# Maxima of the last 64 queries in one block-diagonal product, a slot softmax with other operations, and new order numbers for the attention stage

## The chip, the cores and the metric

One core of a Trainium2 chip runs the whole program. The time is the device time of one execution in microseconds (us). Five engines work side by side: TensorE (PE, with its weight loads as PEld), VectorE (DVE), ScalarE (ACT), GpSimd (POOL) and SyncE (SP, which issues the DMAs).

## The reference, cut to what matters

Attention over 4 batches with 8 heads, 1152 tokens and head size 64, the queries averaged in pairs to 576; then a soft mixture of experts with 32 slots; then a dense layer pair with `h - tanh(h)` between.

```python
q_pool = q.reshape(B, H, S // 2, 2, D).mean(axis=3)
scores = scale * np.matmul(q_pool, k.transpose(0, 1, 3, 2))
scores = scores - np.max(scores, axis=-1, keepdims=True)
attn = np.exp(scores); attn = attn / (np.sum(attn, axis=-1, keepdims=True) + 1e-09)
x = attn @ v                                   # [2304, 512] after the heads are laid side by side
logits = x @ phi                               # 32 slots
d = softmax over tokens (axis 0); slot_input = d.T @ x
slot_out[e] = relu(slot_input[e] @ w1[e]) @ w2[e]
c = softmax over slots (axis 1);  x = c @ slot_out
h = x @ w_in;  out = (h - tanh(h)) @ w_out
```

## The kernel before, in words

**Pairs and steps.** Two heads of one batch form a pair: head 0 lies in partitions 0 to 63, head 1 in 64 to 127. There are 16 pairs, four to a batch. A pair has 18 steps: two halves of 288 queries, nine chunks of 128 keys each. One step of `attend` computes the scores of its chunk for both heads (L556, eight matmuls, which are four products of 64x128 weights per head that use half of the array's rows each, so that the two heads run side by side), takes the exponential on ACT (L568), adds it to a running sum on POOL (L609, on DVE in the last pair) and multiplies it with V (L590, four matmuls per step, each using half of the array's columns). The products with V are issued for 2, 2, 2, 2 and 1 steps at a time (`PV_END`), so five groups to a half. `normalise` sums the running sums over the partitions (L633) and divides.

**Maxima.** The largest score of each query must be known before its scores are computed, because it enters them as the fourth product (`one`, `MX`). `smax` finds it one pair ahead: for each of five blocks `t` of 128 queries and three thirds `g` of the keys it computes the scores of both heads coarsely (L464, two matmuls side by side) and reduces each head's on DVE (L478). 576 queries are four and a half blocks, so the fifth block starts at query 448 and repeats 64 queries of the fourth. `smax_end` reduces over the thirds (L491), transposes (L494) and writes the rows with ten small DMAs a pair (L501): six for the first part (blocks 0 to 2), four for the second (blocks 3 and 4).

**Tiling modes.** TensorE thus works in different shapes of the array: 64x128 (L556, L464), 128x64 (L590, L633), 128x32 (L699, L805, L809) and the full array, 128x128 (L784, L733).

**Slots.** After each batch `moe_batch` computes the logits (L699), an online softmax over tokens (`mx`, `ee`, `ssum`), transposes x and the exponentials (L784, L733), adds to the slot inputs (L805, L809), and makes the softmax over slots for the second use: `c1` (L826 maximum, L827 subtraction), `c2` (L832 exponential), `c3` (L838 sum, L839 plus 1e-9, L840 reciprocal, L841 multiplication). The last batch ends in `combine`. `convert` (L996 to L1030) turns the float64 weights of the last layer into float32 during attention, 32 pieces, and keeps the split form in memory.

**What sets the order.** Nothing in the attention stage is issued in program order. Each piece of work is an `op` with the engines it can run on, a cost, the slots of memory it needs (seven PSUM banks `ps`, with caps of `st` 6 for scores, `sm` 4 for maxima and `ms` 4 for the rest; eight buffers `P` of exponentials) and a number `prio`. `Plan.run` plays the whole stage through on paper: an engine that is free takes the ready op of the lowest number, and on PE, among ops within `SLACK` of the lowest, one that needs no change of mode. A change of mode costs `TURN` on paper. The order so found is written out as each engine's fixed queue; on the chip only semaphores hold it up. Numbers count steps (pair i begins at 18 i) plus an offset from `PR`: the scores of step s stand at s - 2.62, the products with V at s + 0.73.

**After attention** (from L1203) come the expert weights' products (L1251, L1330), whose weights are loaded by DMA as buffers come free, and the dense layers (L1460, L1505).

Of the kernel before, what the change touches and what calls it, by code (L numbers as in the profile page):

```python
# [32 lines left out]
class Plan:  # L33
# [15 lines left out]
    TURN = 190.0  # L49
# [7 lines left out]
    def op(self, engs, fn, prio, deps=(), take=(), use=(), dma=0, alone=None,  # L57
           mode=None):

        o = {
            "n": len(self.ops), "engs": engs, "fn": fn, "prio": prio, "take": tuple(take),
            "use": tuple(use), "dma": dma, "deps": 0, "next": [], "done": False, "alone": alone, "mode": mode,
            "ready": dict.fromkeys(engs, 0.0),
        }
# [20 lines left out]
    def run(self):  # L87
# [20 lines left out]
        while left:  # L108
            progress = True
            while progress:  # L110
                progress = False
                for e in engines:
# [48 lines left out]
                    free_at[e] = end = now + o["engs"][e]  # L161
                    if e == "PE" and o["mode"] not in (None, self.mode):
                        self.mode = o["mode"]
                        free_at[e] = end = end + self.TURN
# [30 lines left out]
def fused_kernel(  # L195
# [12 lines left out]
    nc = tc.nc  # L208
# [39 lines left out]
    PB = 8  # L248
    NXT = 5
    PV_END = (1, 3, 5, 7, 8)  # L250
    CAP_ST, CAP_SM, CAP_MS = 6, 4, 4
    PR = {
# [5 lines left out]
    }  # L258
    tags_w = [f"W{n}" for n in range(NWR)]
    tags_b = [f"B{n}" for n in range(21)]  # L260
# [44 lines left out]
    mrun = cp.tile([128, 2], F32, name="mrun")  # L305
# [11 lines left out]
    MT = [mo.tile([128, 32], F32, name=f"mt{n}") for n in range(4)]  # L317
    one = mo.tile([128, 128], F32R, name="one")
    LOC = ((0, 64), (64, 128))

    def halves(tag):
# [3 lines left out]
    P_buf = [x for n in range((PB + 1) // 2) for x in halves(tags_b[(14, 15, 16, 20, 21)[n]])]  # L325
# [4 lines left out]
        "mc": 2, "k": 1, "v": 2, "q": 1, "rs": 1, "raw": 1, "cv": 1, "x": 1, "cw": 1, "hl": 1,  # L330
    }, PR["sw"])
# [12 lines left out]
    def act(n, sb=0, ptr=0):  # L344
        return {"ACT": 0.8333 * n + 51 + 42 * sb + 93 * ptr}
# [4 lines left out]
    def pool_tt(n):  # L350
        return {"POOL": 2.11 * n + 147}
# [50 lines left out]
    def split(i, what, out, parts, prio):  # L402
# [4 lines left out]
        for n, (c, end, key) in enumerate(parts):  # L407
# [17 lines left out]
            lo = op({"DVE": 1.0417 * w + (700 if i else 67)}, fl, prio + PR["lo"] + (0 if i else PR["late"]), deps=[hi], use=[sl])  # L425
# [20 lines left out]
    QOFF = (0, 128, 256, 384, NQ - 128)  # L446
    PARTS = ((0, 1, 2), (3, 4))
    mc_t, mx_t, mx_m = {}, {}, {}

    def smax(i, part, t, g, prio):  # L450
        a = i % 2
# [3 lines left out]
        msl, n0 = mc_t[i, part], PARTS[part].index(t)  # L455
        c0, q0 = g * KW, QOFF[t]
        deps = ready[i, "k", g][0] + ready[i, "q", 0][0]
        if q0 + 128 > HQ:
            deps = deps + ready[i, "q", 1][0]
        bk = [psum("sm") for _ in range(2)]  # L460

        def f(_):
            for (lo, hi), (ps, _) in zip(LOC, bk):
# [7 lines left out]
        m = op(pe(171), f, prio, deps=deps + mx_m[i, part][:1], mode=ROW2,  # L471
               take=both + ([msl] if first else []), use=both + [msl])
        mx_m[i, part].append(m)
        for h, (ps, pst) in enumerate(bk):
            n = h * len(PARTS[part]) + n0

# [5 lines left out]
            mx_t[i, part].append(op(dve(KW), red, prio, deps=[m], use=pst + [msl]))  # L482

    def smax_end(i, part, prio):
        a = i % 2
        w = len(PARTS[part])
# [3 lines left out]
        def f1(_):  # L490
            nc.vector.tensor_reduce(  # L491
                out=mn[:, 0:2 * w], in_=msl.tile[:, 0:2 * w], axis=AX.X, op=ALU.max, negate=True
# [3 lines left out]
        def f4(_):  # L496
            m = MX[a].bitcast(F32)
            for h in range(2):
                for n, t in enumerate(PARTS[part]):
                    b0 = 2 if t == 4 else 0  # L500
                    nc.sync.dma_start(  # L501
                        out=m[64 * h:64 * h + 1, QOFF[t] + 32 * b0:QOFF[t] + 128],
                        in_=mt[32 * b0 + h * w + n:128:32, :],
                    )

        o1 = op(dve(150), f1, prio, deps=mx_t.pop((i, part)), use=[msl])
# [3 lines left out]
        ready[i, "m", part] = op({"SP": 600.0 * 2 * w}, f4, prio, deps=[o1] + war, dma=4000)  # L510

    def prepare(i, g0):
        def at(key):
            return g0 + PR[key] + (0 if i else PR["first"])

        load(i, "k", at("k"))
        load(i, "q", at("q") - (0 if i else 10))
        load(i, "v", at("v"))
        sum_q(i, at("sum"))
        a = i % 2  # L520
        if i:
            split(i, "q", (QH[a], QL[a]), ((0, NQ, (0, 1)),), at("q0"))
            split(i, "k", (KH[a], KL[a]), ((0, CK, (0, 1, 2)),), at("k0"))
        else:
            split(i, "q", (QH[a], QL[a]), ((0, HQ, (0,)), (HQ, NQ, (1,))), at("q0"))
            split(i, "k", (KH[a], KL[a]), [(g * KW, g * KW + KW, (g,)) for g in range(3)], at("k0"))
        n = 0
        for t in range(3):
            for g in range(3):
                smax(i, 0, t, g, at("m0") + PR["m0d"] * n)  # L530
                n += 1
        smax_end(i, 0, at("e0"))
        for n in range(6):
            smax(i, 1, 3 + n // 3, n % 3, at("m1") + PR["m1d"] * n)
        smax_end(i, 1, at("e1"))
# [5 lines left out]
    def attend(i, s):  # L541
        a = i % 2
        hf, c = divmod(s, NCH)
        g = i * NSTEP + s
# [19 lines left out]
        m = op(pe(520), mm, g + PR["st"], deps=deps, take=both, use=both, mode=ROW2)  # L564
        last_read.setdefault((i, "T"), []).append(m)
        for h, (st, stt) in enumerate(bk):
# [5 lines left out]
            exps.append(op(act(HQ), ef, g + PR["ex"], deps=[m] + exps, take=[] if h else [psl],  # L572
# [7 lines left out]
        if c in PV_END:  # L580
# [4 lines left out]
            def pvf(_):  # L585
# [10 lines left out]
                pe(490 * len(run)), pvf, g + PR["pv"],  # L596
# [17 lines left out]
        if i == NPAIR - 1:  # L614
            engs = dve(2 * HQ)
        acc_last[i, hf] = op(
            engs, add, g + PR["add"],
            deps=exps + (e0 if c == 1 else [acc_last[i, hf]]),
            take=[acc] if c == 1 else [], use=[acc, psl] + ([p0] if c == 1 else []))

    def normalise(i, hf, prio):
# [39 lines left out]
        def ev(_):  # L661
            nc.scalar.activation(out=posl.tile, in_=pvs.tile[:, :HQ], func=AF.Copy)

        oe = op(act(HQ), ev, prio + PR["ev"], deps=[o_pv[i, hf]], take=[posl], use=[pvs, posl])
        o = op(pe(490), sums, prio, deps=[acc_last[i, hf]], take=pst, use=pst + [acc], mode=COL2)
        acc_read[i, hf] = o
        o = op(act(HQ, 0, 1), ln, prio, deps=[o], take=[rsl], use=pst + [rsl])
        o = op(act(HQ, 1), rc, prio, deps=[o], use=[rsl])
        o = op(dve(HQ), n1, prio, deps=[o], use=pst + [rsl])
        o = op(dve(HQ), n2, prio, deps=[o], use=pst + [rsl])  # L670
        xdone.append(
            op(dve(HQ), n3, prio, deps=[o, oe], take=[] if hf else [xsl],
# [10 lines left out]
    def moe_batch(b, g0, dg, last):  # L683
# [5 lines left out]
        prio = [g0 + n * dg for n in range(12)]  # L689
        kinds = ("ms", "sm", "st", "ms", "sm", "st", "ms", "ms") if last else ("ms",) * 8  # L690
        (psL, ptL), (psT, ptT), (psU, ptU), (psS, ptS) = (psum(kinds[n]) for n in range(4))
        new, old = mrun[:, b % 2:b % 2 + 1], mrun[:, 1 - b % 2:2 - b % 2]
# [917 lines left out]
```

## Time and profile before

| | us |
|---|---|
| median of 3 runs | 757.57 |
| the runs | 755.52 to 760.40 |
| span of the profiled execution (first to last instruction; the page gives it no other time) | 753.6 |
| busy PE, DVE, ACT, POOL in the span | 726.4, 652.8, 485.9, 379.8 |

Attention fills the span up to about 470 us, the experts up to about 530 us, and the dense layers the rest. A busy share of an engine says that something was under way on it, not that it was at its peak: a matmul's row lasts longer than the distance to the next one, since they are pipelined. So distances on PE are read from start to start.

### The profile page before, as it was taken

To read this page: it belongs to the slowest core of one execution; us is meant where nothing else is said; L and a number is where in the kernel's file an instruction comes from. 1 tells how busy PE (TensorE), PEld (TensorE's weight loads), DVE (VectorE), ACT (ScalarE), POOL (GpSimd) and SP (SyncE) were. 2 spreads that over 40 slices of the span, in tenths; PEclk is the share of its full clock that TensorE was granted. 3 is DMA by queue.
4 is the path that set the end of the run, shared out by engine and by line. 5 is a ranking of instruction groups with operands and counts; after the bars stand their busy time and mean duration, and the time that the engine had idled before them with its cause. 6 is when DMAs were issued, how large, how long until landed. Compare 5 with 4: busy or idle time off the path is not lost.

```text
span 753.6 us, 16227 instructions
## 1 busy us (share of the span) xinstructions
PE 726.4 (96%) x5977; PEld 512.1 (68%) x5977; DVE 652.8 (87%) x1161; ACT 485.9 (64%) x1050; POOL 379.8 (50%) x275
## 2 busy tenths in 40 slices
PE   6999999999999989999989999998899999999998
PEld 3666666666666656666656666355678888888886
DVE  7999989898999999998989986513999999999994
ACT  1565666565666565666556666314878888888882
POOL 2699999969999869999939960000000000000000
PEclk9999999999999999999989999999799999999999
DMA  6445373453454444464444532999631010101001
GB/s 219 151 159 160 141 230 122 143 152 112 164 182 147 145 154 164 154 205 146 168 171 183 174 140 97 356 409 371 232 145 42 1 43 0 43 1 42 8 35 42
DMA packets 33551, 108.41 MB, mean 144 GB/s; under 512 B 5312, under 2 KB 6208, under 8 KB 33472
## 3 DMA queue, kind: packets, MB, share of 16 engines
q1 hardware_dynamic: 33472, 107.37, 40.5%
q8 instruction: 47, 0.77, 0.4%
q14 instruction: 32, 0.26, 0.1%
HBM read 90.24 MB, written 16.25 MB: 141 GB/s over the span
## 4 chain that ended last, share of the span: by engine, by line
PE 83%; DVE 7%; ACT 3%; POOL 3%; issue 2%; DMA 1%; SPq 0%; DVEq 0%; POOLq 0%; ACTq 0%
PE bk L1505 26%; PE bk L556 21%; PE bk L590 18%; PE bk L464 7%; POOL rt L609 3%; DVE mc L478 2%; PE h L1460 2%; PE bk L633 2%; PE bk L1330 2%; PE bk L1251 2%; DMA rt<-in_moe_w_in_dram 1%; PE bk L699 1%; PE bk L805 1%; PE bk L809 0%; DMA rt<-in_k_dram 0%
## 5 line engine op out<-in xcount | busy, mean ns | idle before, releaser
L609 POOL TENSOR_TENSOR rt<-rt 128x576 f32<-128x576 f32 x240 | 355.7, 1486 | 49.0 <-ACT rt L568 34.5
L568 ACT ACTIVATE rt<-bk 128x288 f32<-128x288 f32 x576 | 204.0, 412 | 147.1 <-PE bk L556 138.2
L478 DVE TENSOR_REDUCE mc<-bk 128x1 f32<-128x384 f32 x480 | 234.4, 546 | 26.3 <-PE bk L464 25.6
L556 PE MATMUL bk<-rt 64*128 64x288 f32 x1728 | 179.3, 310 | 4.8 <-DVE mc L478 4.6
L590 PE MATMUL bk<-rt 128*64 128x288 f32 x1152 | 173.3, 419 | 0.0
L556 PEld LDWEIGHTS bk<-rt 64*128 64x128 f32 x1728 | 138.8, 187 | 47.5 <-DVE mc L478 18.9
L1505 PE MATMUL bk<-rt,gh 128*128 128x512 f32 x576 | 145.3, 396 | 5.0 <-ACT gh L1495 5.0
L1505 PEld LDWEIGHTS bk<-rt,gh 128*128 128x128 f32 x576 | 109.4, 191 | 29.2 <-ACT gh L1495 6.7
L590 PEld LDWEIGHTS bk<-rt 128*64 128x64 f32 x1152 | 70.1, 136 | 55.7 <-issue 25.9
L464 PE MATMUL bk<-rt 64*128 64x384 f32 x480 | 100.1, 395 | 7.9 <-DVE rt L414 7.0
L556 PE MATMUL bk<-rt,one 64*128 64x288 f32 x576 | 91.0, 294 | 0.0
L464 PEld LDWEIGHTS bk<-rt 64*128 64x128 f32 x480 | 54.5, 194 | 47.3 <-issue 18.9
L1505 PE MATMUL bk<-rt,gl 128*128 128x512 f32 x288 | 81.8, 395 | 0.0
L1505 PEld LDWEIGHTS bk<-rt,gl 128*128 128x128 f32 x288 | 54.4, 191 | 9.9 <-DVE gl L1498 0.6
L556 PEld LDWEIGHTS bk<-rt,one 64*128 64x128 f32 x576 | 60.1, 187 | 0.0
L1467 ACT ACTIVATE u<-h 128x768 f32<-128x768 f32 x48 | 39.2, 816 | 27.9 <-PE h L1460 27.9
L1492 DVE COPY_PREDICATED m<-big,th 128x768 f32<-128x768 uint32 x48 | 51.4, 1070 | 0.0
L1481 DVE TENSOR_TENSOR m<-u,th 128x768 f32<-128x768 f32 x48 | 45.6, 951 | 6.4 <-ACT th L1470 6.3
L417 DVE TENSOR_TENSOR rt<-rt 128x576 fp32r<-128x576 f32 (+3 forms) x35 | 47.0, 1343 | 4.4 <-ACT rt L412 4.3
L1498 DVE TENSOR_TENSOR gl<-m,gh 128x768 fp32r<-128x768 f32 x48 | 45.7, 952 | 1.5 <-ACT gh L1495 1.5
L1484 DVE TENSOR_TENSOR th<-h,th 128x768 f32<-128x768 f32 x48 | 45.6, 951 | 0.0
L1495 ACT ACTIVATE gh<-m 128x768 fp32r<-128x768 f32 x48 | 40.9, 852 | 7.3 <-DVE m L1492 5.0
(136 smaller groups left out, 695.6 us busy)
## 6 DMA issues: line engine op xcount, KB each, us to landing
rt<-in_moe_w_dram SPq DMA_DIRECT2D x64, 512.0 KB
rt<-in_v_dram SPq DMA_DIRECT2D x16, 576.0 KB
rt<-in_k_dram SPq DMA_DIRECT2D x15, 576.0 KB
rt<-in_q_dram SPq DMA_DIRECT2D x15, 576.0 KB
rt<-in_moe_w_in_dram SPq DMA_DIRECT2D x16, 512.0 KB
rt<-in_moe_w_out_dram SPq DMA_DIRECT2D x16, 512.0 KB
wo_hl<-rt SPq DMA_DIRECT2D x16, 512.0 KB
rt<-wo_hl SPq DMA_DIRECT2D x16, 512.0 KB
```

The source lines that it names most:

```text
L417: nc.vector.tensor_tensor(out=lo_t[:, c:end], in0=sl.tile[:, c:end], in1=hi_t.bitcast(F32)[:, c:end], op=ALU.subtract,)
L464: nc.tensor.matmul(out=ps.tile[:, :KW], lhsT=QH[a][lo:hi, q0:q0 + 128], rhs=KH[a][lo:hi, c0:c0 + KW],)
L478: nc.vector.tensor_reduce(out=msl.tile[:, n, g:g + 1], in_=ps.tile[:, :KW], axis=AX.X, op=ALU.max)
L556: nc.tensor.matmul(out=st.tile[:, :HQ], lhsT=w[lo:hi, k0:k0 + 128], rhs=x[lo:hi, q], start=(n == 0), stop=(n == 3),)
L568: nc.scalar.activation(out=psl.tile[:, h, :], in_=st.tile[:, :HQ], func=AF.Exp, scale=ESC)
L590: nc.tensor.matmul(out=pvs.tile[lo:hi, :HQ], lhsT=vt[:, cc, h, :], rhs=p.tile[:, h, :], start=(cc == 0), stop=(cc == NCH - 1),)
L609: eng.tensor_tensor(out=acc.tile, in0=p0.tile if c == 1 else acc.tile, in1=psl.tile, op=ALU.add)
L1481: nc.vector.tensor_tensor(out=m.tile, in0=u.tile, in1=th.tile, op=ALU.mult)
L1484: nc.vector.tensor_tensor(out=v(th), in0=hp_(), in1=v(th), op=ALU.subtract)
L1492: nc.vector.copy_predicated(m.tile, big.tile.bitcast(U32), th.tile)
L1498: nc.vector.tensor_tensor(out=lo.tile, in0=m.tile, in1=hi.tile.bitcast(F32), op=ALU.subtract)
L1505: nc.tensor.matmul(out=acc[t].tile, lhsT=l.tile[:, x * TB + t * 128:x * TB + (t + 1) * 128], rhs=got[f + x][:, c:c + DM], start=(f == 0 an ...
```

## The change

**Maxima.** The fifth block is now the last 64 queries alone (`TAIL`). A new tile `QD` of 128x128 holds head 0's 64 queries in the upper left block and head 1's in the lower right, zero elsewhere (`both_heads`, two ACT copies a pair). One product of the full array per third gives 64 rows for each head, in place of two products of half the rows, and one reduction follows in place of two. `smax_end` handles 6 and 3 columns in place of 6 and 4 and still issues ten DMAs.

**Slots.** `c1` to `c6`: the subtraction, the sum with 1e-9 and the multiplication move from DVE to ACT, as five exponentials with a bias and five scalings per batch; the running maximum and sum are joined by reductions over neighbouring columns and one ACT operation.

**Order.** Every op gets a number of its own (`PT`, about 280 of them, for the first pair and the others apart); `TURN` depends on the mode turned to; costs of ACT and POOL on paper are raised; the plan lets DVE's subtraction in `split` and POOL exclude each other (`lock`). The groups of V (`PV_END`), the buffers and the caps stay. The DMA scratch is made smaller, and some tiles and tags are added.

```diff
-    TURN = 190.0
+    TURN = {"64x128": 207.0, "128x64": 143.0, "128x128": 150.0, "128x32": 150.0}
...
+                    if o["lock"] and e == "DVE":
+                        end = max(now, free_at["POOL"]) + o["engs"][e]
+                        free_at[e] = free_at["POOL"] = end
...
+    SLACK = 0.84
+    ADD_DVE = ()
+    PT = {
...
+        "mm": [-0.2, -16.17, 1.4, 2.07, -227.31, 4.18, 6.57, 7.07, 8.23, 11.43, 15.34, 11.32,
+            7.8, -97.33, -113.2],
...
+        "st": [-2.03, -1.94, -1.25, -0.84, -0.92, -0.65, 1.04, 2.04, 2.05, 2.96, 5.34, 6.94,
+            7.08, 10.16, 8.47, 10.62, 12.56, 14.19],
...
+        "pv": [67.2, 31.7, 119.17, 177.75, 142.36, 6.22, 6.06, 15.07, 7.0, 184.4, 14.88, -137.07,
+            65.75, 35.64, 16.43, 14.69, 60.93, 17.39],
...
     def act(n, sb=0, ptr=0):
-        return {"ACT": 0.8333 * n + 51 + 42 * sb + 93 * ptr}
+        return {"ACT": 0.8333 * n + 68 + 42 * sb + 93 * ptr}
...
-        return {"POOL": 2.11 * n + 147}
+        return {"POOL": 2.32 * n + 147}
...
+    def both_heads(i, prio):
+        sl, loads = kvq[i, "q"]
+
+        def f(_):
+            for h, (lo, hi) in enumerate(LOC):
+                nc.scalar.activation(
+                    out=QD[lo:hi, 64 * h:64 * h + 64], in_=sl.tile[lo:hi, TAIL:NQ], func=AF.Copy)
+
+        ready[i, "d", 0] = [
+            op({"ACT": 330.0}, f, prio, deps=[loads[-1], consts["m"]] + tail_m, use=[sl])]
+        tail_m.clear()
...
-        bk = [psum("sm") for _ in range(2)]
+        bk = [psum("sm") for _ in range(1 if tail else 2)]
...
+            for (lo, hi), (ps, _) in zip(((0, 128),) if tail else LOC, bk):
                 nc.tensor.matmul(
-                    out=ps.tile[:, :KW], lhsT=QH[a][lo:hi, q0:q0 + 128],
-                    rhs=KH[a][lo:hi, c0:c0 + KW],
+                    out=ps.tile[:, :KW], rhs=KH[a][lo:hi, c0:c0 + KW],
+                    lhsT=QD if tail else QH[a][lo:hi, q0:q0 + 128],
                 )
...
-        m = op(pe(171), f, prio, deps=deps + mx_m[i, part][:1], mode=ROW2,
+        m = op(pe(171), f, prio, deps=deps + mx_m[i, part][:1], mode=FULL if tail else ROW2,
                take=both + ([msl] if first else []), use=both + [msl])
...
         def c1(_):
-            lt = lt_t[b][:, 0:5]
-            mx_ = mo.tile([128, 5, 1], F32, tag="mx", name="mx", bufs=1)
-            nc.vector.tensor_reduce(out=mx_, in_=lt, axis=AX.X, op=ALU.max)
-            nc.vector.tensor_tensor(
-                out=lt, in0=lt, in1=mx_.to_broadcast([128, 5, NS]), op=ALU.subtract
-            )
+            bx["mx"] = m = mo.tile([128, 5, 1], F32, tag="mx", name="mx", bufs=1)
+            nc.vector.tensor_reduce(
+                out=m, in_=lt_t[b][:, 0:5], axis=AX.X, op=ALU.max, negate=True)
 
         def c2(_):
+            for t in range(5):
+                lt = lt_t[b][:, t]
+                nc.scalar.activation(out=lt, in_=lt, func=AF.Exp, bias=bx["mx"][:, t])
+
+        def c3(_):
+            bx["sm"] = sm = mo.tile([128, 5, 1], F32, tag="smx", name="smx", bufs=1)
+            nc.vector.tensor_reduce(out=sm, in_=lt_t[b][:, 0:5], axis=AX.X, op=ALU.add)
+
+        def c4(_):
             nc.scalar.activation(
-                out=lt_t[b][:, 0:5], in_=lt_t[b][:, 0:5], func=AF.Exp)
...
-            nc.vector.tensor_scalar(out=sm, in0=sm, scalar1=1e-9, scalar2=None, op0=ALU.add)
-            nc.vector.reciprocal(out=sm, in_=sm)
-            nc.vector.tensor_tensor(
-                out=lt, in0=lt, in1=sm.to_broadcast([128, 5, NS]), op=ALU.mult
-            )
+                out=bx["sm"], in_=bx["sm"], func=AF.Relu, bias=eps[:, 0:1])
+
+        def c5(_):
+            nc.vector.reciprocal(out=bx["sm"], in_=bx["sm"])
+
+        def c6(_):
+            for t in range(5):
+                lt = lt_t[b][:, t]
+                nc.scalar.activation(out=lt, in_=lt, func=AF.Relu, scale=bx["sm"][:, t])
...
+    nc = _bacc.Bacc(
+        "TRN2", target_bir_lowering=False, num_devices=1, dynamic_dma_scratch_size=1024)
```

## Rows read from the trace of the kernel before

**Rows 1.** Busy time by stretch: stretch, length; PE, PEld, DVE, ACT, POOL; clock, DMA share, GB/s.
```profile
208.00:236.00 28.00, 28.00 (x274) 18.70 (x272) 25.61 (x52) 17.45 (x47) 26.90 (x19) 1.00 0.45 154
...
376.00:404.00 28.00, 25.77 (x207) 15.93 (x206) 22.68 (x47) 17.09 (x46) 14.77 (x11) 0.88 0.56 210
```

**Rows 2.** Waits from 20 to 460 us: waiter, awaited: us in total, times, longest.
```profile
PE bk L556 <- DVE mc L478: 4.6, 3, 2.2
...
DVE mc L478 <- PE bk L464: 25.6, 41, 2.7
```

**Rows 3.** Groups of instructions: shapes, count | busy us, mean ns | idle before.
```profile
L478 DVE TENSOR_REDUCE mc<-bk 128x1 f32<-128x384 f32 x480 | 234.4, 546 | 26.3 <-PE bk L464 25.6
...
L745 ACT ACTIVATE et<-bk 64x32 f32<-64x32 f32 x4 | 0.8, 192 | 0.1
```

**Rows 4.** Chain that ended last, in time order: start us, us, what.
```profile
42.20 1.42 POOL rt L609
43.70 1.41 POOL rt L609
...
178.78 1.84 PE bk L556 x21
...
204.74 1.71 PE bk L556 x21
...
595.55 4.10 PE bk L1505 x18
```

**Rows 5.** PE in time order, start us, us, instruction: products with V and neighbours.
```profile
254.95 0.34 PE L464 MATMUL bk<-rt 64*128 64x384 f32 x2
255.22 1.19 PE L590 MATMUL bk<-rt 128*64 128x288 f32 x8
256.34 0.66 PE L556 MATMUL bk<-rt 64*128 64x288 f32 x6
256.83 0.29 PE L556 MATMUL bk<-rt,one 64*128 64x288 f32 x2
256.97 0.34 PE L464 MATMUL bk<-rt 64*128 64x384 f32 x2
257.14 0.56 PE L556 MATMUL bk<-rt 64*128 64x288 f32 x6
257.54 0.29 PE L556 MATMUL bk<-rt,one 64*128 64x288 f32 x2
...
454.36 2.16 PE L590 MATMUL bk<-rt 128*64 128x288 f32 x16
456.45 0.67 PE L556 MATMUL bk<-rt 64*128 64x288 f32 x6
```

**Rows 6.** PE in time order: two visits of the full array, among 64x128 work.
```profile
259.20 1.53 PE L784 MATMUL bk<-ident,xT 128*128 128x128 f32 x12
260.66 0.67 PE L556 MATMUL bk<-rt 64*128 64x288 f32 x6
...
266.73 0.39 PE L464 MATMUL bk<-rt 64*128 64x384 f32 x2
267.09 0.66 PE L784 MATMUL bk<-ident,xT 128*128 128x128 f32 x4
267.68 0.40 PE L556 MATMUL bk<-rt 64*128 64x288 f32 x1
```

**Rows 7.** DVE in time order: the last step of a slot softmax.
```profile
383.72 1.37 DVE L841 TENSOR_TENSOR lt<-lt,smx 128x160 f32<-128x160 f32 x1
```

**Rows 8.** PE in time order: the slot inputs' products of two batches.
```profile
271.19 1.06 PE L805 MATMUL bk<-rt,et 128*32 128x512 f32 x8
272.09 1.02 PE L809 MATMUL bk<-x,et 128*32 128x512 f32 x2
...
387.19 1.93 PE L805 MATMUL bk<-rt,et 128*32 128x512 f32 x8
388.91 1.92 PE L809 MATMUL bk<-x,et 128*32 128x512 f32 x2
```

More of the change, by code (lines that the diff above doesn't have):

```diff
@@ L57, in op @@
     def op(self, engs, fn, prio, deps=(), take=(), use=(), dma=0, alone=None,
-           mode=None):
+           mode=None, lock=False):
         o = {
@@ L400, in load, with split @@
                    dma=nb))
-    def split(i, what, out, parts, prio):
+    def split(i, what, out, parts, prio, plo):
         sl, loads = kvq[i, what]
@@ L424, in split @@
                     use=[sl])
-            lo = op({"DVE": 1.0417 * w + (700 if i else 67)}, fl, prio + PR["lo"] + (0 if i else PR["late"]), deps=[hi], use=[sl])
+            lo = op(dve(w), fl, plo, deps=[hi], use=[sl],
+                    lock=i > 0)
             split_done[:] = [lo]
@@ L497, in f4 @@
             m = MX[a].bitcast(F32)
-            for h in range(2):
-                for n, t in enumerate(PARTS[part]):
-                    b0 = 2 if t == 4 else 0
+            for n in range(w):
+                for h in range(2):
+                    tail = part and n == 2
+                    if n % 2 != h and not tail:
+                        continue
+                    c = TAIL if tail else 128 * (3 * part + n // 2)
                     nc.sync.dma_start(
-                        out=m[64 * h:64 * h + 1, QOFF[t] + 32 * b0:QOFF[t] + 128],
-                        in_=mt[32 * b0 + h * w + n:128:32, :],
+                        out=m[64 * h:64 * h + 1, c:c + (64 if tail else 128)],
+                        in_=mt[64 * h + 2:64 * h + 64:32, :] if tail else mt[n:128:32, :],
                     )
-        o1 = op(dve(150), f1, prio, deps=mx_t.pop((i, part)), use=[msl])
+        o1 = op(dve(200), f1, prio, deps=mx_t.pop((i, part)), use=[msl])
         if i == 0:
@@ L688, in moe_batch, with p @@
         bx = {}
-        prio = [g0 + n * dg for n in range(12)]
+        def p(n):
+            return at(g0, ("ml" if last else "mo", n))
         kinds = ("ms", "sm", "st", "ms", "sm", "st", "ms", "ms") if last else ("ms",) * 8
         (psL, ptL), (psT, ptT), (psU, ptU), (psS, ptS) = (psum(kinds[n]) for n in range(4))
-        new, old = mrun[:, b % 2:b % 2 + 1], mrun[:, 1 - b % 2:2 - b % 2]
+        new, old = mrun[:, 2 * b + 3:2 * b + 4], mrun[:, 2 * b + 1:2 * b + 2]
         parts = ((0, 1, 2), (3,)) if last else ((0, 1, 2, 3),)
@@ L864, in moe_batch @@
-        osum = op(dve(600), ssum, prio[3], deps=[oe, oa])
-        if not last:
-            for t in range(1, 5):
-                xtok((t,), parts[0], prio[2 + t])
-        os_ = op(pe(1740), slots, prio[7], deps=[ocp] + xo, take=ptS, use=ptS + [xb], mode=COL4)
+            xtok((0, 1), parts[1], (p(12), p(13)))
+            xtok((2, 3), parts[1], (p(14), p(15)))
+            xtok((4,), parts[1], (p(16), p(17)))
+        om = op(dve(213), mx, p(18), deps=[oL], use=ptL)
+        om = op(dve(30 if b == 0 else 140), mx2, p(18), deps=[om])
@@ new lines, in moe_batch @@
+        oe = op(act(192, 0, 1), ee, p(19), deps=[om], use=ptL)
+        oa = op(act(1, 1, 1), ea, p(20), deps=[om])
+        ot = op(pe(220), tr("E", psT), p(21), deps=[oe], take=ptT, use=ptT, mode=FULL)
+        ocp = op(act(260), cp_e, p(22), deps=[ot], use=ptT)
+        osum = op(dve(150), ssum, p(23), deps=[oe])
+        osum = op(dve(170), ssum2, p(24), deps=[osum])
+        if b:
+            osum = op(act(1, 1, 1), srun_, p(25), deps=[osum, oa])
+        if not last:
+            for t in range(5):
+                xtok((t,), parts[0], (p(t), p(t + 5)))
```

262 lines of the change are left out of this document (128 added, 134 removed), and 48 rows, old and new, of tables (PR, PT).

## The prediction

> **What bounds the kernel now.** I read four views in this order. First, busy time by stretch: in an undisturbed stretch of attention PE shows 28.00 us of 28, POOL 26.90 and DVE 25.61 [rows 1], so three engines compete and shares alone decide nothing. Second, the waits: PE stood still for DVE's maxima for 4.6 us in all, in three waits of up to 2.2, while DVE stood still for PE 41 times, 25.6 us in all [rows 2]. Who waits for whom says that PE is the bound and DVE is not. Third, the chain that ended last: the same piece of PE comes back after 204.74 - 178.78 = 25.96 us in a plain pair, and POOL starts an addition every 43.70 - 42.20 = 1.50 us; 17 of them (16 additions, one sum of queries) make 25.5 us a pair [rows 4]. So POOL is 0.4 us a pair behind PE: it becomes the bound as soon as PE gets more than that. Fourth, PE in order of time, from start to start, to see what it does with a time that has no gaps [rows 5, 6].
>
> **What a change of mode costs.** From half rows (L464) to half columns (L590) the start comes after 0.27 us where the same L464 ahead of an L556 takes 0.17: 0.10. Eight products with V before half rows take 1.12, sixteen take 2.09, so eight in mode take 0.97: 0.15 for the way back. The first six L556 after it take 0.49 instead of 0.40: 0.09 [rows 5]. A visit of the half-column mode thus costs 0.34 us beside its work. From 255.22 to 454.36 [rows 5] I count, with both of these, 66 visits in 6.75 pairs, 9.8 a pair. For the full array: L464 to L784 is 0.36 instead of 0.17, 0.19; twelve transposes and the way back take 1.46, four 0.59, so one takes 0.109 and the way back 0.15 [rows 6]; with the 0.10 of the first products after it, a visit alone costs 0.44. Between a half-column visit and the way back it adds 0.15 at least, since the rest is paid anyway.
>
> **The change part by part.**
>
> *Reductions.* 48 of 480 go (three a pair): 48 x 0.546 = 26.2 us of DVE [rows 3]. DVE waits for PE, so none of it is on the path except the 4.6 us counted below; I take zero, and as ends zero and the 26.2 less those 4.6 if DVE held PE in ways that the waits don't show.
>
> *Products of the tail.* Three pairs of half-row products (0.17 each [rows 5]) become three full-array ones. The nearest row of a full-array product of this type is L1505: 18 of 512 columns in 4.10, so 0.228, and 0.171 for 384 [rows 4]. Nothing gained or lost. But they need the full array's mode. Their numbers (7.8, -97.33, -113.2) let two go as soon as the first product of block 3 is through, on the banks left; the third waits for a bank. So I take two visits a pair, one alone and one beside V: 0.44 + 0.15 = 0.59, 16 pairs: **+9.4**. Ends: one visit beside V, 16 x 0.15 = 2.4; three alone, 48 x 0.44 = 21.1.
>
> *Order of V.* The scores' numbers now lie between -2 and 14 in a pair, while four of the ten groups of V have numbers far above the group that follows (31.7 and 177.75 before 6.22; 15.07 before 7.0; 65.75 before 16.43; 60.93 before 17.39). Such a group is held back until nothing else is ready, and the next then follows in the same mode: (3, 5), (7, 8), (12, 14), (16, 17). Ten groups and two sums make twelve; less four, 8 visits; less the 2.2 merges that there are now, 5.8. I take 7: 2.8 x 0.34 x 16 = **-15.2**. Ends: 0 (9.8 again) and 4.0 x 0.34 x 16 = -21.8. Together with the tail this is -0.36 us a pair, just under POOL's 0.4.
>
> *Slot softmax.* In the second and third batch PE waits for maxima that queue on DVE behind L841, 1.37 us [rows 7] for a 160-column product: nearly all of the 4.6 us [rows 2]. After the last of these waits PE's clock is granted at 0.88 over the stretch [rows 1], and L805 and L809 take 1.93 and 1.92 us against 1.06 and 1.02 in the batch before [rows 8], the lower of the two levels (1.2 of 2.4 GHz): 1.8 us. L841, L839 and L827 leave DVE, so **-6.4**. Ends: zero, if other DVE work takes their place before the maxima, and -6.4. What is late next is the POOL addition behind ACT.
>
> *ACT.* 32 copies for QD and some eleven small operations a batch more, at 0.192 [rows 3]: 32 x 0.192 + 44 x 0.192 = 14.6 us, at 17.45 of 28 busy [rows 1]. Zero; if the cover went, the copies of the first pair and the last softmax would show, under 1 us.
>
> *At zero.* The maxima's DMAs stay ten a pair on SP, in another cut; three more memsets on POOL come before its first work; the first scores wait for 18 reductions as now; the conversions of the last weights, pushed back in number, have DVE's new room; if they ran over the end, a tail of at most a few of them (2 to 3 reductions' length each) would hold the last buffers. Scratch, tags and longer tiles move no instruction. The experts and dense layers come after, unchanged.
>
> **Sum.** -6.4 + 9.4 - 15.2 = -12.2 on the profiled execution's 753.6: 741.4. That execution is known by its span alone, 4.0 below the median of the runs, 757.57; with the same 4.0 the forecast is **745.4 us**.
>
> **The rivals.**
>
> 1. *Slower: the tails go alone and V is not merged.* Place: between half-row products, where the plan finds PE without ready scores. Price 48 x 0.44 = 21.1, less 6.4: 753.6 + 14.7 + 4.0 = 772.3. It decides once the tails' visits cost more than 6.4 us plus what merged V gives, so from 15 lone visits on if V keeps its 9.8. For it: numbers as scattered as these say little of which op meets which, and the third tail is always late. Against: the plan is told of the price, 150 for turning to the full array and 207 for going back, and this is near the 0.44 of the rows.
> The Trainium skill, TensorEngine Tiling (Array Packing), Key Properties, says that changing the tiling mode drains TensorE. By that rule each tail outside the half-row mode pays again, which speaks against this part of the change; the rows' 0.34 and 0.44 agree.
>
> 2. *No change: POOL holds the pairs.* Additions and sums on POOL are as many as before. If the lock between POOL and DVE or a late exponential costs 0.4 us a pair, the merged V is lost and the tail's cost hidden; what is left is the softmax: 753.6 - 6.4 + 4.0 = 751.2. For it: POOL at 26.90 of 28. Against: it idles around the batches (14.77 of 28 [rows 1]), where PE's gain counts in full.
>
> 3. *Much faster.* 5.8 visits and tails beside V: (21.8 - 2.4) / 16 = 1.2 us a pair for PE. Twelve plain pairs fall by POOL's 0.4 (4.8), the other 0.8 (9.7) takes work of the batches, the four batch pairs fall by 1.2 (4.8), the softmax gives 6.4: -25.7, 731.9.
>
> 4. *The change does not do what it says.* A full-array product at twice its price would add 48 x 0.17 = 8 us; L1505's row excludes it.
>
> **How the numbers follow.** Forecast 0.40, rival 3 0.12, rival 2 0.29, rival 1 0.19. The likeliest case has 741 to 750 as its own range. The whole range, 732 to 768, reaches down to rival 3 and up towards rival 1, whose centre it leaves out; the lower half of rival 1, with fewer lone visits, is in it. A measurement of this kernel tells about 1% (7.6 us) from no change: faster (under 750) 0.52, the forecast and rival 3; within 0.29, rival 2; slower 0.19, rival 1.
>
> **What would show it.** L590's rows: fewer, longer runs (x12, x16), about 7 visits a pair, or the order's step is wrong. The tail's products in PE's time order: in pairs or beside L590, or each alone with 0.2 us before and after. PE's wait for L478 near zero, and the clock at 1.00 through the third batch. DVE's idle time for PE well above 25.6 us. A plain pair at 25.5 to 25.7 us between equal pieces, with POOL near 17 x 1.50. It would be wrong if PE shows new waits for ACT or POOL, if conversions run past the last pair, or if plain pairs get longer.

## The result and the profile after

The changed kernel takes 750.36 us, the median of four runs (748.09 to 751.34), against 757.51 for the kernel before in runs beside it (755.52 to 760.4): a ratio of 0.9903, with a 95% interval of 0.9874 to 0.9932. That is 7.15 us less, where 12.2 had been forecast (745.4 us). It lies inside the range, 0.4 us past the end of the likeliest case's own, and so near the bound of 1% that faster by over 1% and within 1% can't be told apart. The profiled execution took 748.09 us with a span of 746.3, 7.3 less than the span before. Of the runs of the kernel before that were made beside the experiments, those with a mean granted clock of 0.986 or less took 757.5 to 761.5 us and those with 0.991 or more 754.5 to 757.2, while the changed kernel's four runs all show 0.993, so a part of the difference between medians is clock.

By stage, from the starts of the experts' first product (L1251, now L1340) and of their last (L1316, now L1405): attention ends 9.2 us earlier (477.96 to 468.72), the experts take 2.6 more (46.3 to 48.9), the dense layer 0.7 less (229.4 to 228.7).

The same stretches after the change, read as in [rows 1] (stretch, length; PE, PEld, DVE, ACT, POOL; clock, DMA share, GB/s), with the start of the experts at the end:

```profile
208.00:236.00 28.00, 27.93 (x270) 18.46 (x268) 25.97 (x55) 19.48 (x53) 25.69 (x19) 1.00 0.59 201
...
376.00:404.00 28.00, 27.82 (x261) 17.95 (x259) 20.14 (x43) 21.04 (x65) 22.58 (x17) 1.00 0.32 121
468.70:490.00 21.30, 21.28 (x184) 7.81 (x188) 6.06 (x21) 8.69 (x26) 0.00 (x0) 0.92 0.84 332
```

The undisturbed stretch looks much as it did. The stretch of the third batch is the one that changed: PE works 27.82 us in place of 25.77, at the full clock in place of 0.88.

The waits from 20 to 460 us (waiter, awaited: us in total, times, longest), which answer to [rows 2]:

```profile
DVE mc L553 <- PE bk L537: 37.3, 58, 2.8
...
PE bk L537 <- DVE rt L1102: 0.5, 1, 0.5
...
PE bk L634 <- DVE mc L553: 0.4, 2, 0.3
PE bk L537 <- DVE mc L553: 0.4, 1, 0.4
```

PE's 4.6 us behind the maxima are down to 0.8 (1.9, in five waits, when the changed kernel was run again), and DVE's idle time for PE has grown from 25.6 to 37.3.

The groups of instructions (shapes, count | busy us, mean ns | idle before), as in [rows 3]; the first two are of the whole span, the others from 20 to 470 us:

```profile
L687 POOL TENSOR_TENSOR rt<-rt 128x576 f32<-128x576 f32 x240 | 344.7, 1461 | 61.1 <-ACT rt L646 51.0
...
L553 DVE TENSOR_REDUCE mc<-bk 128x1 f32<-128x384 f32 x432 | 215.2, 549 | 38.5 <-PE bk L537 37.3
```

```profile
L537 PE MATMUL bk<-rt,qd 128*128 128x384 f32 x45 | 14.0, 391 | 0.1
...
L914 ACT ACTIVATE lt<-lt,mx 128x32 f32<-128x32 f32 x20 | 4.7, 313 | 3.6 <-DVE mx L908 3.5
L930 ACT ACTIVATE lt<-lt,smx 128x32 f32<-128x32 f32 x15 | 3.6, 346 | 0.0
```

All 48 reductions are gone. The tail's products are single instructions of the full array (the first pair's three lie before 20 us). The softmax's new ACT steps take 313 and 346 ns each, not the 192 of [rows 3]. From 20 to 460 us PE waits for none of them; VectorE waits for the exponentials, 2.2 us in two waits.

PE in order of time (start us, us, instruction), as in [rows 5, 6, 8]: two tails between half-row work, a third next to the products with V, then the slot inputs of the third batch and the experts' first block:

```profile
210.04 0.44 PE L537 MATMUL bk<-rt 64*128 64x384 f32 x2
210.41 0.61 PE L537 MATMUL bk<-rt,qd 128*128 128x384 f32 x2
...
211.68 0.45 PE L537 MATMUL bk<-rt,qd 128*128 128x384 f32 x1
212.05 1.19 PE L668 MATMUL bk<-rt 128*64 128x288 f32 x8
...
382.97 1.06 PE L888 MATMUL bk<-rt,et 128*32 128x512 f32 x8
383.87 1.02 PE L892 MATMUL bk<-x,et 128*32 128x512 f32 x2
...
468.72 5.34 PE L1340 MATMUL bk<-rt,siT 128*32 128x512 f32 x32 [0.38 <-DVE siT L1035]
```

The third batch's products take 1.06 and 1.02 us, where [rows 8] had 1.93 and 1.92. From the first score product to the first of the experts, PE turns to half columns 151 times, 9.4 a pair (155 before, counted the same way). It makes 23 visits of the full array for the tails, 6 of them alone among half-row work and 17 next to another mode.

DVE through the third batch's slot softmax, answering to [rows 7]:

```profile
379.27 0.32 DVE L908 TENSOR_REDUCE mx<-lt 128x5 f32<-128x160 f32 x1
...
382.13 0.32 DVE L918 TENSOR_REDUCE smx<-lt 128x5 f32<-128x160 f32 x1 [1.14 <-ACT lt L914]
382.36 1.01 DVE L553 TENSOR_REDUCE mc<-bk 128x1 f32<-128x384 f32 x2
383.29 0.18 DVE L925 RECIPROCAL smx<-smx 128x5 f32<-128x5 f32 x1
```

No step there takes 1.37 us any more, and maxima go between the steps.

### The profile page after: what moved, and what is told of

Its sections match the earlier page's. It is cut to its first block, busy times and chain, and to the rows that moved or that the text cites. A ratio compares the mean times of both kernels' runs of the same rounds, so it can differ in the third digit from the quotient of the medians.

```text
span 746.3 us, 15967 instructions
## 1 busy us (share of the span) xinstructions
PE 722.7 (97%) x5929; PEld 506.2 (68%) x5929; DVE 620.6 (83%) x1097; ACT 499.3 (67%) x1124; POOL 368.1 (49%) x278
## 4 chain that ended last, share of the span: by engine, by line
PE 78%; DMA 8%; DVE 6%; ACT 3%; POOL 2%; issue 2%; SPq 0%; DVEq 0%; ACTq 0%; POOLq 0%
PE bk L1594 26%; PE bk L634 19%; PE bk L668 17%; PE bk L537 6%; DMA rt<-in_moe_w_dram 4%; DVE mc L553 3%; PE h L1549 2%; POOL rt L687 2%; PE bk L1340 2%; PE bk L711 2%; DMA rt<-in_moe_w_out_dram 2%; DMA rt<-in_moe_w_in_dram 1%; PE bk L867 1%; PE bk L780 1%; ACT u L1556 1%
## 5 line engine op out<-in xcount | busy, mean ns | idle before, releaser
L687 POOL TENSOR_TENSOR rt<-rt 128x576 f32<-128x576 f32 x240 | 344.7, 1461 | 61.1 <-ACT rt L646 51.0
L553 DVE TENSOR_REDUCE mc<-bk 128x1 f32<-128x384 f32 x432 | 215.2, 549 | 38.5 <-PE bk L537 37.3
L668 PE MATMUL bk<-rt 128*64 128x288 f32 x1152 | 171.2, 418 | 0.0
L634 PEld LDWEIGHTS bk<-rt 64*128 64x128 f32 x1728 | 137.8, 187 | 48.0 <-DVE mc L553 18.0
L537 PE MATMUL bk<-rt 64*128 64x384 f32 x384 | 79.3, 394 | 8.4 <-DVE rt L473 6.5
L537 PEld LDWEIGHTS bk<-rt 64*128 64x128 f32 x384 | 41.9, 193 | 38.2 <-DVE mc L553 11.4
L1576 DVE SCALAR_TENSOR_TENSOR m<-y,m 128x768 f32<-128x768 f32 x48 | 45.6, 951 | 0.3
```

The costliest lines, as they stand in the source:

```text
L537: nc.tensor.matmul(out=ps.tile[:, :KW], rhs=KH[a][lo:hi, c0:c0 + KW], lhsT=QD if tail else QH[a][lo:hi, q0:q0 + 128],)
L553: nc.vector.tensor_reduce(out=msl.tile[:, n, g:g + 1], in_=ps.tile[:, :KW], axis=AX.X, op=ALU.max)
L634: nc.tensor.matmul(out=st.tile[:, :HQ], lhsT=w[lo:hi, k0:k0 + 128], rhs=x[lo:hi, q], start=(n == 0), stop=(n == 3),)
L668: nc.tensor.matmul(out=pvs.tile[lo:hi, :HQ], lhsT=vt[:, cc, h, :], rhs=p.tile[:, h, :], start=(cc == 0), stop=(cc == NCH - 1),)
L687: eng.tensor_tensor(out=acc.tile, in0=p0.tile if c == 1 else acc.tile, in1=psl.tile, op=ALU.add)
```

## The experiments

Two theories stood against each other. **A**, that of the forecast: PE is the bound of attention, so the mode visits decide. **B**: only the softmax's waits were won, and the pairs are held by something else, POOL to begin with. Where an order is called kept, every queue issues in the order of the kernel that was edited. Intervals are of the ratio to the kernel before.

### The slot softmax

**e1_old_softmax** puts the three steps that ACT had got back on VectorE in the changed kernel, with one exponential for the five; the sum with 1e-9, the reciprocal and the multiplication follow the sum at its place in the queue:

```
-  tensor_reduce(out=m, in_=lt_t[b][:, 0:5], op=ALU.max, negate=True)
+  tensor_reduce(out=m, in_=lt, op=ALU.max)
+  tensor_tensor(out=lt, in0=lt, in1=m.to_broadcast([128, 5, NS]), op=ALU.subtract)
...
+  tensor_scalar(out=sm, in0=sm, scalar1=1e-9, scalar2=None, op0=ALU.add)
+  reciprocal(out=sm, in_=sm)
+  tensor_tensor(out=lt, in0=lt, in1=sm.to_broadcast([128, 5, NS]), op=ALU.mult)
```

> The changed kernel with its order kept and the slot softmax of before put back on DVE (subtraction, sum with 1e-9, reciprocal and multiplication; one exponential on ACT). Theory A, the stalls of PE behind DVE's slot softmax were most of the gain (4.6 us of waits and 1.8 us of halved clock): it gives back 4 to 6.4 us, 754 to 757. Theory B, the new order alone took the stalls away, since DVE has room now: under 1.5 us, 750 to 752, and PE waits for L553 under 1 us.

Measured: 755.16 us (0.9972, 0.9953 to 0.9991); the changed kernel, run again beside it as **after_again**, took 750.53 (0.991, 0.9886 to 0.9934).

> The changed kernel once more, for the comparisons of this group: 748 to 752 by every theory.

So 4.6 us come back, as theory A had it. DVE, POOL and PE of e1 around its second batch, in order of time:

```profile
269.11 1.36 DVE L910 TENSOR_TENSOR lt<-lt,mx 128x160 f32<-128x160 f32 x1
270.39 1.47 DVE L553 TENSOR_REDUCE mc<-bk 128x1 f32<-128x384 f32 x3
...
272.13 1.17 DVE L921 TENSOR_SCALAR smx<-smx 128x5 f32<-128x5 f32 x1
...
273.55 0.33 DVE L923 TENSOR_TENSOR lt<-lt,smx 128x160 f32<-128x160 f32 x1
```

```profile
266.13 7.13 POOL L687 TENSOR_TENSOR rt<-rt 128x576 f32<-128x576 f32 x5 [0.82 <-ACT rt L646]
274.30 1.41 POOL L687 TENSOR_TENSOR rt<-rt 128x576 f32<-128x576 f32 x1 [1.04 <-ACT rt L646]
```

```profile
270.99 1.12 PE L867 MATMUL bk<-ident,xT 128*128 128x128 f32 x8 [1.02 <-DVE mc L553]
...
274.40 0.44 PE L537 MATMUL bk<-rt 64*128 64x384 f32 x1 [1.38 <-DVE mc L553]
```

A product of 160 columns takes 1.36 us while POOL adds, and 0.33 in the gap of POOL from 273.26 to 274.30. Five numbers a row (L921) take 1.17 us and end as POOL's additions end. PE then stands for the maxima behind them, 1.02 and 1.38 us. The rule of the Trainium skill (SBUF — State Buffer, SBUF: two separate sides) is that one pair of ports is shared by GpSimd and by those VectorE operations that have two inputs in SBUF or run in a mode that takes both ports, as a lock held for a whole instruction. By that rule such a short operation waits out the addition, and these rows agree. Not every step was held up: the sum over 160 columns, a reduction at 271.79, took 0.30 us while POOL added.

**e2_no_softmax_tail** takes away from the kernel before, its order kept, the three steps that ACT got:

```
-  tensor_tensor(out=lt, in0=lt, in1=mx_.to_broadcast([128, 5, NS]), op=ALU.subtract)
...
-  tensor_scalar(out=sm, in0=sm, scalar1=1e-9, scalar2=None, op0=ALU.add)
...
-  tensor_tensor(out=lt, in0=lt, in1=sm.to_broadcast([128, 5, NS]), op=ALU.mult)
```

> The kernel before with its order kept; of the slot softmax the subtraction (L827), the sum with 1e-9 (L839) and the multiplication (L841) are left out, so their DVE time alone goes. Theory A, PE's stalls stood behind them: 4.6 to 6.4 us faster than before, 751 to 753, with the clock at 1.00 in the third batch. Theory B, the maxima queue there for other reasons (the order): under 1.5 us.

Measured: 749.87 us (0.9902, 0.988 to 0.9925), 8.6 less than the 758.44 beside it, a little more than theory A had asked for. PE's waits in it:

```profile
PE bk L633 <- POOL rt L609: 3.8, 3, 1.3
...
PE bk L556 <- DVE mc L478: 0.2, 1, 0.2
```

The wait for maxima goes from 4.6 to 0.2. Waits for POOL's last addition of a pair are what is late next: three of them, where the kernel before has one of 1.4 us.

**e10_slots_alone** does the change's slot softmax alone on the kernel before, with its order and its half-row tails. It differs from the change in small things: no 1e-9 on the sum, the running sum joined as before, and the scaling issued behind the next copy on ACT.

```
-  tensor_tensor(out=lt, in0=lt, in1=sm.to_broadcast([128, 5, NS]), op=ALU.mult)
+  def scale():
+      for t in range(5):
+          scalar.activation(out=lt_t[b][:, t], in_=lt_t[b][:, t], func=AF.Relu, scale=sm[:, t])
+  scale() if last else later.append(scale)
```

> The kernel before with its order and its half-row tails kept, and the slot part alone changed: subtraction and scaling on ACT (the scaling is issued behind the next copy of attention's output), maxima joined by reductions, the sum with 1e-9 dropped since a sum of at least 1 does not change by it in float32. Theory B', the slot part is the whole gain and tails and order cancel: 749 to 752, like the changed kernel. Theory A', the order gave some of it: 753 to 755.

Measured: 752.65 us (0.993, 0.9911 to 0.9949), 5.35 less than the 758.0 beside it. What the tails and the new order add to that is the rest to 750.5, some 2 us, and the two intervals overlap. So this decides neither for B' nor for A'. In the profiled executions, attention from its first score product to the experts' first product takes 452.3 us in e10 and 447.5 and 449.1 in the changed kernel's two; there the tails and the order may be worth 3 to 5 us, part of which the later stages take back.

### The tails

**e4_tail_alone** puts the block-diagonal product into the kernel before, order kept. The reduction that goes is replaced by a copy of one column, and the DMA scratch is the smaller one.

```
-  for (lo, hi), (ps, _) in zip(LOC, bk):
+  for (lo, hi), (ps, _) in zip(((0, 128),) if t == 4 else LOC, bk):
-      lhsT=QH[a][lo:hi, q0:q0 + 128], rhs=KH[a][lo:hi, c0:c0 + KW]
+      lhsT=QD[a] if t == 4 else QH[a][lo:hi, q0:q0 + 128], rhs=KH[a][lo:hi, c0:c0 + KW]
...
+  if t == 4 and n == 3: tensor_copy(out=msl.tile[:, n, g:g + 1], in_=eps); return
```

> The kernel before with its order kept and only the tail's product changed: one block-diagonal product of the full array for two half-row products, one reduction of 384 columns and a tiny copy for two reductions, two ACT copies a pair. No other order number is new, so each tail is a visit of its own where the old products stood. Theory A, PE is the bound and the rows' price holds: 48 visits at 0.15 to 0.44, 7 to 21 us slower, 764 to 778. Theory E, DVE's relief (about 19 us net) is worth something in waits that PE's long rows hide: between 3 us faster and 5 us slower, 754 to 762.

Measured: 766.44 us (1.0121, 1.0098 to 1.0145), 8.0 more. Its tails' products and its reductions from 20 to 480 us:

```profile
L487 DVE TENSOR_REDUCE mc<-bk 128x1 f32<-128x384 f32 x409 | 203.7, 549 | 42.6 <-PE bk L470 41.9
...
L470 PE MATMUL bk<-rt,qd 128*128 128x384 f32 x45 | 18.0, 432 | 0.0
```

From the first score product on they make 36 visits, 6 between half-row products (two of these together with transposes) and 30 next to another mode: by the prediction's prices 6 x 0.44 + 30 x 0.15 = 7.1 us, against 8.0. The 8.0 is the whole edit's: VectorE's relief and the copies on ACT are in it, and the granted clock is at the lower level for 10.3 us of attention, where the kernel before has 6.9. So the price fits, but it is not measured by itself.

**e3_tail_halfrow** leaves the changed kernel and its order as they are but makes the tail's product one of half rows, so that no tail needs the full array.

```
-  for (lo, hi), (ps, _) in zip(((0, 128),) if tail else LOC, bk):
+  for (lo, hi), (ps, _) in zip(((0, 64),) if tail else LOC, bk):
-      lhsT=QD if tail else QH[a][lo:hi, q0:q0 + 128]
+      lhsT=QD[lo:hi, :] if tail else QH[a][lo:hi, q0:q0 + 128]
```

> The changed kernel with its order kept, the tail's product made in the half-row mode (64 of QD's rows; head 1's tail maxima are left out), so no full-array visit is left for it. Theory A, PE is the bound and a change of mode costs what the rows said (23 visits: 6 alone at 0.44, 17 beside other modes at 0.15): 5.2 us faster than the changed kernel, 743 to 747. Theory C, POOL holds the pairs and hides it: under 1.5 us, 749 to 751.

Measured: 753.26 us (747.11 to 758.15 in 12 runs; 0.9937, 0.9908 to 0.9966). The 23 visits are gone, 5.2 us by the prices, and the median has not fallen; neither range holds it. But it is no clean reading of the visits: the runs spread over 11 us, and in the profiled execution, of 748.54 us, PE waits 1.26 us for a maximum at 88.58 and the granted clock is at 0.5 from 91.0 to 94.4. A gain of some 2 us may be hidden in this, and the 5.2 are not there. That the visits are off the path that sets the end is the likelier reading, not a shown one.

### The order of V

**e9_pv3** gives V in three groups a half instead of five and has the order planned again:

```
-  PV_END = (1, 3, 5, 7, 8)
+  PV_END = (2, 5, 8)
```

> The changed kernel with the products with V in groups of three steps in place of two, the plan run anew on the same numbers: about 102 half-column visits in place of 151. Theory A as predicted, a visit fewer is 0.34 us less: 49 x 0.34 = 17 us faster, 733 to 736. Theory D, scores and V then wait for each other (eight P buffers, exponentials in threes) and the numbers fit one set of groups only: slower by 10 to 25 us, 760 to 775, with waits on PE where there were none.

Measured: 763.91 us (1.0086, 1.0065 to 1.0107), 13.4 more than the changed kernel, with 102 turns to half columns instead of 151. Its products with V in all:

```profile
L668 PE MATMUL bk<-rt 128*64 128x288 f32 x1152 | 161.2, 416 | 0.0
```

V's products take 161.2 us of rows where the changed kernel has 171.2. But from the start of one score product to the next one right behind it there are 0.076 us on average instead of 0.071, between two products with V 0.116 instead of 0.112, and between two products for maxima 0.093 instead of 0.038. Counted from the starts, some 25 us went into such small delays (10.4, 4.4 and 10.4). Most of them lie under the rows: the waits that the profile shows for PE add up to 5.6 us. The order and the times at which V's data are asked for changed too, so e9 shows that fewer turns are not enough, as theory D had it, not that they are worth nothing.

### One engine after another

Each of these kernels takes work from one engine and keeps the order. What they leave out is in the expectations.

**e7_pe_relief** (changed kernel, one of four score products left out: 576 x 0.065, some 37 us of PE, six taking 0.40 in [rows 5]):

```
-  terms = ((KL[a], QH[a]), (KH[a], QL[a]), (KH[a], QH[a]), (one, MX[a]))
+  terms = ((KH[a], QL[a]), (KH[a], QH[a]), (one, MX[a]))
```

> The changed kernel with its order kept; the first of the four products of each score step (low part of K by high part of Q) is left out: 288 x 0.13 = 37 us less for PE and nothing else. Theory A, PE is the bound: 20 us or more faster, 720 to 731, until POOL's 25.5 us a pair stops it. Theory C, POOL and the exponentials behind it hold the pairs: under 8 us, 743 to 751. A mixture, where each engine holds some stretches: 10 to 18 us, 732 to 741.

**e6_pool_relief** (changed kernel, POOL's additions cut to 192 of 288 columns behind the first):

```
-  out=acc.tile, in0=p0.tile if c == 1 else acc.tile, in1=psl.tile
+  w = HQ if c == 1 else 192
+  out=acc.tile[:, :, :w], in0=(p0 if c == 1 else acc).tile[:, :, :w], in1=psl.tile[:, :, :w]
```

> The changed kernel with its order kept; 14 of 16 additions a pair on POOL (and those of the last pair on DVE) take 192 of 288 columns for each head, so a third of these sums is left out: some 210 x 0.45 = 95 us less POOL. Theory C, POOL holds the pairs: 8 to 25 us faster, 725 to 742. Theory F, after PE's relief gave 1.6 us: no engine alone holds them, each fixed queue waits for the others in turn: under 5 us, 745 to 751.

**e5_dve_relief** (kernel before, the maxima of block 4 read 128 of 384 columns; e11 does this to block 3 of the changed kernel):

```
-  tensor_reduce(out=msl.tile[:, n, g:g + 1], in_=ps.tile[:, :KW], ...)
+  tensor_reduce(out=msl.tile[:, n, g:g + 1], in_=ps.tile[:, :128 if t == 4 else KW], ...)
```

> The kernel before with its order kept; block 4's reductions (L478, 96 of 480) read 128 of 384 columns, so two thirds of those scores are left out of the maxima: 96 x 0.27 = 26 us less DVE, as much as the change takes away, with no mode, no copy and no order changed. Theory A, DVE only waits for PE: 0 to 1.5 us faster, 756 to 758. Theory E, DVE holds PE in small waits that the rows hide: 4 to 10 us faster, 747 to 753.

**e8_pe_pool_relief** is e7 and e6 together, **e11_three_relief** these two and DVE.

> Both reliefs at once, order kept: one score product in four and a third of the additions left out. Theory C: as POOL's relief alone plus what PE then gives, 20 to 40 us faster, 710 to 730. Theory F with DVE as the third: the maxima and conversions on DVE, at 25 of 28 us, keep it within 12 us of the changed kernel, 738 to 750.

> As with both reliefs, and block 3's reductions on DVE read 128 of 384 columns (26 us less DVE), order kept. Theory F, the three are bound jointly: at least 15 us faster than the two reliefs together, 705 to 730. If the queue of the conversions' loads, one raw buffer, holds DVE and with it the rest: within 5 us of them.

| kernel | taken off | us | against its base | ratio to before |
|---|---|---|---|---|
| e7 | PE, 37 us | 748.95 | -1.6 | 0.9902 (0.9869 to 0.9934) |
| e6 | POOL, 89 us | 752.2 | +1.7 | 0.9923 (0.9895 to 0.995) |
| e5 | DVE, 25 us | 754.64 | -3.8 | 0.9966 (0.9944 to 0.9987) |
| e8 | PE and POOL | 743.06 | -7.5 | 0.9785 (0.9742 to 0.9828) |
| e11 | PE, POOL and DVE | 737.01 | -13.5 | 0.9723 (0.9692 to 0.9754) |

The base is the changed kernel at 750.53, for e5 the kernel before at 758.44; the intervals of e7 and e6 hold its ratio of 0.991, so neither is told from no change. e6 lies just above the range of theory F. e5 lies between its two ranges, and its profiled execution, at 758.17 us, doesn't show where the 3.8 come from. The undisturbed stretch of e7, and its longest waits of PE for the maxima and for VectorE's conversions of the last weights (L1102):

```profile
208.00:236.00 28.00, 27.55 (x216) 16.60 (x216) 25.59 (x50) 17.54 (x49) 22.56 (x16) 0.94 0.56 195
```

```profile
PE bk L537 <- DVE mc L553: 4.1, 4, 1.6
PE bk L634 <- DVE mc L553: 3.1, 6, 0.9
PE bk L537 <- DVE rt L1102: 2.5, 3, 1.6
```

With a fifth fewer products in it, PE still shows 27.55 us of 28. Part of what was taken away came back as waits: for maxima 0.8 us in the changed kernel and 7.2 here, of all kinds 1.3 and 14.4. The granted clock was at 0.5 for 13.7 us of attention, which by an estimate took back up to another 6.9. The rest of the 37 lies inside the rows. The weight loads (PEld) show it better: 16.60 against 18.46. The Trainium skill (Perfetto Trace Analysis, Identifying the Most-Contended Engine) says that the busy time of products is no good measure for TensorE, since they are pipelined, and that the share of the peak and the weight loads' share are to be read instead. These two rows agree.

POOL's additions in e6 (a group of the whole span), its waits in e8, and DVE's in e8 and e11:

```profile
L688 POOL TENSOR_TENSOR rt<-rt 128x384 f32<-128x384 f32 (+1 forms) x240 | 255.9, 1086 | 143.8 <-ACT rt L646 128.8 <-PE bk L713 10.7
```

```profile
POOL rt L688 <- ACT rt L646: 113.3, 45, 9.0
...
DVE bk L1089 <- DMA rt<-in_moe_w_in_dram: 9.9, 7, 2.6
DVE bk L1089 <- DMA rt<-in_moe_w_out_dram: 9.5, 6, 2.3
```

```profile
DVE mc L553 <- PE bk L537: 34.5, 44, 1.9
...
DVE bk L1089 <- DMA rt<-in_moe_w_out_dram: 9.2, 6, 2.7
DVE bk L1089 <- DMA rt<-in_moe_w_in_dram: 7.9, 6, 2.5
```

What POOL gains it spends waiting for exponentials: 89 us shorter, 82.7 us more idle. POOL alone is not the bound either. Only with PE and POOL relieved together does the time fall by more than the measurement's width. With DVE relieved too the median is 6.0 lower, where a joint bound of the three was expected to give at least 15; the two intervals overlap and one of e8's four runs took 735.54 us, so DVE's part is not told from zero. In both, DVE waits longer for the weights that it converts in its spare time: 19.4 and 17.1 us, 6.3 in the changed kernel.

## Why the prediction was near, and where it failed

**Slot softmax, -6.4: right.** The wait (4.6 to 0.8), the clock (0.88 to 1.00) and the products behind it came as written. The size is 4.6 us by e1, which has the loss behind the last batch (below) in it, 5.35 by e10, 8.6 by e2, where nothing is put on ACT. By e1 and e10 this is most of the 7.15.

**ACT at zero: held, but for the last batch.** The new operations cost more than priced (313 and 346 ns), and in attention PE has no wait for them. What they cost behind the last batch stands under the experts below.

**"PE is the bound": the step that failed.** The prediction took PE's 28.00 us of 28 and the one-sided waits as proof. Taking 37 us off PE in the changed kernel gave 1.6, not told from zero. A row of a product is longer than the distance to the next one: two in 0.34 us with the next start after 0.17 [rows 5]. So small waits vanish under the rows, and gaps show only what is left. In plain attention, PE, DVE and POOL stand within a tenth of each other (27.93, 25.97, 25.69 of 28) with queues in a fixed order. What PE or POOL alone gained, it gave back in waits for the others (e7, e6); relieved together, they gained 7.5 us (e8). That these engines and the order hold attention jointly fits this; it isn't shown that nothing else does.

**Order of V, -15.2: not there.** This is the term of the sum that failed. The visits stayed at 9.4 a pair, 9.7 before; 7 were forecast. The held-back groups did not merge as the numbers suggested. And e9, with 6.4 a pair, lost 13.4 us. The count alone brings the term to its end of near zero (155 turns less 151, 4 x 0.34 = 1.4); e9 says that fewer visits would not have given their price by themselves. What the order did was something else: from the first sum (L633, now L711) of one pair to that of the next, four plain pairs (the sixth, seventh, tenth and eleventh, with no slot work of a batch) took 25.8, 25.6, 25.4 and 26.8 us and now take 27.3, 26.4, 27.4 and 28.2, while the two that had held most of the second and third batch's work went from 35.5 and 38.3 to 31.8 and 27.2. Plain pairs that get longer are a sign of being wrong that the prediction had named.

**Tails, +9.4: price near, count wrong, path open.** The edit with 36 visits cost 8.0 us in the old order (7.1 by the prices). The new order has 23, not 32, or 5.2 us by the prices, and e3's median gets none of that back. So the new order takes in tails that cost 8 in the old one. Order and tails together were forecast at -5.8 and measured at about -2, which is not told from zero. That the time still lies in the range is luck in part: of the two terms one was missing and the other too large, with opposite signs, and some 4 of the 5.0 us between forecast and result are what is left of them.

**Reductions at zero: nearly.** 25 us less on DVE gave 3.8 in e5, about a seventh, though [rows 2] showed DVE waiting for PE. In the changed kernel this gain, if it is there, is inside the 2 us.

**The experts, taken as unchanged: +2.6 in the profile.** The first block takes 5.34 us for its 32 products; before it took this:

```profile
477.96 3.64 PE L1251 MATMUL bk<-rt,siT 128*32 128x512 f32 x32 [0.38 <-DVE siT L944]
```

From 469.4 to 472.8 us the granted clock is at 0.5, the lower level; with the same wait of 0.38 us before it, the kernel before had none. That is 1.7 us of the 2.6. It is not the whole cause: run again, the changed kernel kept the full clock there, its first block took 3.64 us, and its experts still took 48.3 us. PE then waits behind that block:

```profile
475.18 0.74 PE L1319 MATMUL bk<-ident,cs 128*128 128x128 f32 x5 [1.11 <-DVE cs L1309]
```

These products need the last batch's slot softmax. POOL has no work by then, and there the new steps are the slower ones: from the maximum (L908) to the first use of the finished softmax (L1307) they take 3.72 us in both profiles of the changed kernel; before (L826 to L1218) they took 2.29. In e1, with the old steps in the new order, it is 2.33 us, PE has no such wait, and the experts take 47.2. So the move to ACT gives back some 1.1 us where VectorE is free.

**The rivals.** Rival 2's 751.2 us is the number nearest to the result, but its mechanism is right in part at most: it had POOL hold the pairs, and e6 gives POOL 89 us without a gain. Once PE is relieved, POOL is one of the things that hold them: e8 lies 5.9 us below e7. Merged V, which POOL was to hide, never came about. What rival 2 had right is that little but the softmax would be left. Rival 1's price, visits that cost time, fits e4, in the old order only. Nothing came of rival 3.

**Open.** Why attention with three engines relieved still ends at 458.6 us (468.7 without): the waits for exponentials and for weights point to the kept order, but no order planned for these shorter times was run. Whether a plan with fewer turns and V's data asked for as early as now would gain is open for the same reason. PE and POOL were relieved in the changed kernel alone, so what would bind the kernel before is shown for VectorE only (e5).

## What to carry to other kernels

Full rows and one-sided waits don't prove that an engine is the bound: take a tenth of its work away with the order kept, then the next engine's, then both, before pricing anything on it. A small operation that queues ahead of work that feeds PE is worth more than its own length, above all where another engine can hold it up; moving three of them won most of what this change won, and lost some 1.1 us in the one batch where nothing held them up. A mode's price need not show in the time: putting 36 visits into one order cost 8 us, and taking 23 out of another won nothing that could be measured. Read a change of order from the order that came out: the count of visits in the new trace settled what its numbers had only suggested.

## What the runs showed of the hardware

- VectorE steps next to POOL's additions took several times their length: 1.36 us for 160 columns and 1.17 for five, against 0.33 for 160 columns in a gap of POOL (e1). That five columns can cost over a microsecond was not expected.
- A relieved PE can lose its clock. In e7 the granted clock was at 0.5, the lower of the two levels, from 100.4 to 103.8, 161.9 to 168.7 and 209.6 to 213.1 us, 13.7 us in all, where the changed kernel's attention has none; each followed a wait of PE for VectorE, of 1.61, 1.39 and 1.64 us, the first two for conversions and the last for maxima (the 0.94 in the row above is the last of these). This too gave back some of the 37 us.
- e4 has two such stretches, 273.3 to 276.7 and 392.7 to 399.6, each at a wait of PE for DVE of some 2.2 us. The kernel before has waits of 2.22 us, up to 270.29, and of 2.23 us, up to 385.61, and lost its clock at the second alone (384.9 to 391.8): a wait of one length did not always cost it.
